# First loads on one queue and a newly searched instruction order in a fused attention and FFT kernel

## The chip, the cores and the metric

The kernel runs on one core of one Trainium2 chip. The metric is device microseconds (us) of one execution; lower is better. A run also reports the span from its first to its last instruction, some 2 us shorter than the time, and the mean clock that the throttle granted TensorE over that span (1.0 is full speed). That clock matters here: all differences in question are a few us, and one stretch of TensorE at half clock (3.41 us in these traces) costs about 1.7.

## The reference, cut to what matters

Branch A is compressive-memory attention: 32 heads of 20 columns, a sequence of 2048 rows in 4 segments of 512, softmax inside the segment and a linear memory from the segments before. Branch B is a 2-D FFT filter of its own input. A gate mixes the two.

```python
def _A_ref(x, wq, wk, wv, wo, beta):          # x: 1 x 2048 x 640, H = 32, N = 4 segments, L = 512
    ...
    for s in range(N):
        qs, ks, vs = (q[:, :, s].copy(), k[:, :, s].copy(), v[:, :, s].copy())
        logits = jnp.einsum('bhqd,bhkd->bhqk', qs, ks) * scale + mask
        p = _softmax(logits, axis=-1)
        a_dot = jnp.einsum('bhqk,bhkd->bhqd', p, vs)
        pq = phi(qs)
        num = jnp.einsum('bhld,bhde->bhle', pq, M)
        den = jnp.einsum('bhld,bhd->bhl', pq, z)[..., None] + 1e-06
        o = g * (num / den) + (1.0 - g) * a_dot
        ...
def _B_ref(x, w_r, w_i):
    X = rfft2(x) * (w_r + 1j * w_i)
    return irfft2(X)
...
g = _sigmoid((x * gate_w).sum(-1, keepdims=True))
return g * a + (1 - g) * b
```

## The kernel before

The program first records every operation (a matmul group, an eviction from PSUM, a mask, a DMA) with its inputs and outputs. A long list of integers, `ORDER`, then gives the order in which each engine issues its operations: entry `v` is operation `v // 2`, and `v % 2` picks one of up to two engines (or DMA queues) that may do it. Semaphore waits are made from the recorded dependences, so another list gives the same result, at another time. The list was found by an off-line search over a model of the durations (`QUEUE` has the model's issue and transfer times of DMAs in ns).

```python
    EARLY = ("ld_wqa", "ld_wka", "ld_wqb", "ld_wkb", "ld_wv", "ld_x", "ld_fcat", "ld_big", "ld_beta", "ld_gw", "ld_hm")
    ...
    def dma(self, dst, src, nbytes, r, w, prio, tr=False, name="", after=(), queue="sp"):
        ...
        queues = ("sp", "act") if name in self.EARLY else (queue,)
        return self.Sc.op({e: (f, cost, 0.0) for e in queues}, r=r, w=w, ...)

    def schedule(self, pools, order, nsem=56):
        for v in order:
            o = ops[v // 2]
            o.eng = list(o.alts)[v % 2]
            queue[o.eng].append(o)
        ...
    def warm_up(self):                       # ten dummy matmuls of 512 columns, before any data are there
        ...
        for k in range(self.NWARM):
            self.mms([(lambda k=k: (self.ps(bank, 0, [1, L]), t.ap(0, [1, P]), t.ap(P, [1, L]), True, True, {}), 1000)],
                     [b("warm"), bank], [], -1.0, name="warm")

    def mask(self, s, g, np_, d0, s0, n, rk, wk, prio, base, step=64):   # GpSimd, causal mask on the exp tile
        e0 = self.exo(s, g)
        self.one("pool", lambda e: e.affine_select(
            self.ex.ap(e0 + d0, [1280, 4], [1, n], np_=np_), self.ex.ap(e0 + s0, [1280, 4], [1, n], np_=np_),
            [[0, 4], [step, n // 64], [1, 64]], ALU.is_ge, 0.0, base=base, channel_multiplier=-1), ...)

    # filter of branch B: the product with the weights, added up by VectorE or GpSimd
    fn = lambda e, ...: e.tensor_tensor(Yt.ap(r * 322, [1, KD]), Pt.ap(a0 * 322, [1, KD]), Pt.ap(a1 * 322, [1, KD]), op)
    self.either(fn, KD, [...], [Yb[r]], prio2, name="W_add")
    # phi of branch A, in two steps on VectorE
    fmax = lambda e: e.tensor_scalar(dst(), qsl(), 0.0, 1.0, ALU.max, ALU.add)          # "phi_max"
```

The scores of the attention come in 92 units (a QK matmul group, then one exp on ACT). I use the starts of these 92 exps, numbered from 0, as milestones.

The softmax here doesn't subtract the row's maximum and nothing guards it: scores larger than these inputs give would overflow.

## Time and profile before

| | before |
|---|---|
| first measurement | 245.87 us median of 3 (243.79 to 251.13) |
| profiled span, clock | 244.7 us, 0.986 |
| TensorE, VectorE, ACT, GpSimd busy | 94%, 81%, 81%, 68% |

The prediction below shows the lines. Two things help in reading on. The profiled execution had one stretch of half clock, 208.3 to 215.2 us. And with 48 runs of this kernel on record with their clock at the end, its runs fall into classes by granted clock: mean span 241.6 us at 0.998 to 1.0 (12 runs), 243.3 at 0.992 to 0.993 (23), 245.0 at 0.985 to 0.986 (11; the five of them in the fast state have 244.6), 247.4 at 0.979 (2, both in the slow state). One window of 3.41 us at half clock takes 0.7% off the mean clock, and from class to class the span grows by about 1.7 us.

### The profile page before, as it was taken

Reading aid. Unit: us, or ns where it says so; the run is one execution under the profiler, and the core shown is the slowest. Engines: PE = TensorE matmul, PEld = TensorE weight load, DVE = VectorE, ACT = ScalarE, POOL = GpSimd, SP = SyncE. Lnnn points to the kernel's source line nnn. Section 1 sums busy time; section 2 is a strip of 40 time slices with the busy share of each in tenths; the row PEclk is TensorE's granted clock in tenths of the full one; section 3 lists DMA queues with packets and bytes.
Section 4 is the critical chain, followed back from the end, with each engine's and each line's share of the span. In section 5 each row is a group of like instructions: output and inputs, shape, how many; then the busy total and the mean of one; then the engine's idle time right before and its main releaser. Section 6 shows DMA issues by size and latency. Waiting matters only on the chain.

```text
span 244.7 us, 10242 instructions
## 1 busy us (share of the span) xinstructions
PE 229.2 (94%) x4347; PEld 141.3 (58%) x4361; DVE 197.3 (81%) x481; ACT 199.3 (81%) x241; POOL 166.5 (68%) x297
## 2 busy tenths in 40 slices
PE   7699999999989999999889999899989999899994
PEld 2476566765556565555546555455545556467794
DVE  0379998879899996898899798998988878635563
ACT  2089688889899999999889979999899978388730
POOL 8514259447959956938964999877899867459730
PEclk9999999999999999999999999999999999599999
DMA  7999859993998775494688571264676995722123
GB/s 174 297 348 206 198 165 175 288 195 100 169 285 175 169 220 147 100 240 89 224 211 250 151 233 50 99 175 138 183 221 198 237 180 101 112 54 86 56 85 108
DMA packets 58928, 42.17 MB, mean 172 GB/s; under 512 B 30020, under 2 KB 55172, under 8 KB 58884
## 3 DMA queue, kind: packets, MB, share of 16 engines
q1 hardware_dynamic: 56100, 39.72, 66.4%
q10 hardware_dynamic: 2784, 1.81, 2.9%
q8 instruction: 34, 0.56, 1.0%
q14 instruction: 10, 0.08, 0.1%
HBM read 23.32 MB, written 12.30 MB: 146 GB/s over the span
## 4 chain that ended last, share of the span: by engine, by line
PE 59%; DVE 14%; DMA 10%; ACT 9%; SPq 3%; issue 2%; ACTq 0%; DVEq 0%
PE psum L514 53%; PE psum L512 7%; ACT ex L1263 6%; DMA xT<-in_A_x_dram 3%; DMA pkn<-phk 2%; SPq L548 2%; DMA r<-r_scr 2%; DVE Pt L1439 2%; DMA qk_scr<-qu 2%; DMA r_scr<-rc 2%; SPq L546 1%; DVE G L1485 1%; DVE phk L1085 1%; DVE oU L1526 1%; ACT et L1072 1%
## 5 line engine op out<-in xcount | busy, mean ns | idle before, releaser
L1284 POOL TENSOR_SCALAR_AFFINE_SELECT ex<-ex 128x256 bf16<-128x256 bf16 (+2 forms) x224 | 122.1, 567 | 41.1 <-ACT ex L1263 37.7
L1263 ACT ACTIVATE ex<-psum 128x2048 bf16<-128x2048 f32 (+4 forms) x92 | 138.7, 1508 | 13.9 <-PE psum L514 12.0
L514 PE MATMUL psum<-qkp 20*64 20x64 bf16 (+5 forms) x1280 | 32.7, 272 | 2.2 <-ACT ex L1263 1.7
L514 PE MATMUL psum<-xT,wk 128*128 128x256 bf16 (+1 forms) x280 | 34.1, 276 | 0.2 <-issue 0.2
L514 PE MATMUL psum<-wv,xT 128*32 128x321 bf16 (+3 forms) x400 | 30.1, 301 | 0.6 <-DVE va L1115 0.3
L514 PE MATMUL psum<-xT,wq 128*128 128x512 bf16 (+1 forms) x121 | 27.5, 396 | 2.6 <-DMA xT<-in_A_x_dram 2.0
L1439 DVE TENSOR_TENSOR Pt<-psum,Wt 128x642 bf16<-128x642 f32 x32 | 25.5, 821 | 2.3 <-PE psum L514 2.1
L514 PEld LDWEIGHTS psum<-qkp 20*64 20x64 bf16 x1280 | 13.5, 103 | 19.5 <-ACT ex L1263 13.6
L514 PEld LDWEIGHTS psum<-xT,wk 128*128 128x128 bf16 (+1 forms) x280 | 20.1, 99 | 6.4 <-issue 0.8
L512 PE MATMUL psum<-wo,oU 128*32 128x320 bf16 x480 | 23.5, 319 | 0.0
L906 POOL TENSOR_TENSOR xsb<-xf 128x320 bf16<-128x320 bf16 (+2 forms) x12 | 9.3, 777 | 17.7 <-DVE xsb L906 13.3
L525 DVE CAST ot<-psum 128x320 bf16<-128x320 f32 x21 | 10.1, 491 | 12.6 <-PE psum L512 10.1
L514 PEld LDWEIGHTS psum<-wv,xT 128*32 128x32 bf16 (+1 forms) x400 | 14.3, 96 | 8.4 <-issue 3.1
L514 PE MATMUL psum<-big,Ac 128*128 128x160 bf16 (+2 forms) x96 | 18.1, 258 | 0.7 <-DVE Pt L1439 0.3
L1115 DVE TENSOR_TENSOR va<-psum,ebx 128x320 bf16<-128x320 f32 x32 | 15.2, 484 | 4.3 <-ACT gate L1113 2.1
L514 PE MATMUL psum<-big,Cp 128*128 128x321 bf16 (+1 forms) x96 | 18.0, 302 | 0.2 <-DVE G L1485 0.2
L514 PE MATMUL psum<-ex,va 128*32 128x64 bf16 (+3 forms) x576 | 17.4, 256 | 0.7 <-DVE dn L1152 0.3
L1485 DVE TENSOR_TENSOR G<-eo,psum 128x320 bf16<-128x320 f32 x32 | 14.7, 482 | 3.6 <-PE psum L514 2.6
L514 PEld LDWEIGHTS psum<-ex,va 128*32 128x32 bf16 x576 | 11.1, 96 | 9.7 <-POOL ex L1284 3.4
L514 PE MATMUL psum<-tt,Yt 128*128 128x256 bf16 (+1 forms) x96 | 16.4, 275 | 0.2
L1072 ACT ACTIVATE et<-qu 128x512 bf16<-128x512 bf16 x25 | 15.6, 629 | 0.1
L512 PEld LDWEIGHTS psum<-wo,oU 128*32 128x32 bf16 x480 | 12.6, 101 | 5.3 <-issue 1.3
(99 smaller groups left out, 393.5 us busy)
## 6 DMA issues: line engine op xcount, KB each, us to landing
qkp<-qk_scr SPq DMA_DIRECT2D x28, 160.0 KB
tt<-tab_tt SPq DMA_DIRECT2D x8, 512.0 KB, 4.3
qk_scr<-qu SPq DMA_DIRECT2D x12, 256.0 KB, 3.1
u_scr<-ub SPq DMA_DIRECT2D x12, 256.0 KB, 3.8
xsb<-in_A_x_dram SPq DMA_DIRECT2D x6, 320.0 KB, 6.3
oU<-u_scr SPq DMA_DIRECT2D x15, 128.0 KB, 2.7
out_dram<-ot SPq DMA_DIRECT2D x12, 160.0 KB
Wt<-in_B_w_r_dram SPq DMA_DIRECT2D x16, 80.2 KB, 2.6
```

Source lines behind the costliest of these rows:

```text
L512: h = e.matmul(dst, wt, r_, start=st, stop=sp_, **{**kw, "tile_position": (0, q), "skip_group_check": True})
L514: h = e.matmul(o_, l_, r_, start=st, stop=sp_, **kw)
L525: alts["dve"] = (lambda e: e.tensor_copy(dst(), src()), 67 + 1.04 * n, 68.0)
L546: return e.dma_start_transpose(d_, s_)
L548: return e.dma_start(d_, s_)
L906: self.either(lambda e, dst=dst, src=src, d0=d0, n=n, op=op: e.tensor_tensor(xs.ap(o + dst, [D, 2], [1, n]), xf.ap(src + d0, [321, 2], [1, ...
L1072: self.one("act", lambda e: e.activation(et.ap(0, [1, L]), qsl(), ACT.Exp), L, [qb], [b("et", pi_)], late, name="phi_exp")
L1115: self.one("dve", lambda e: e.tensor_tensor(va.ap(i * H * VW + h0 * VW, [VW, nh], [1, DH]), self.ps(bank, 0, [DH, nh], [1, DH]), self.ebx. ...
L1263: self.one("act", lambda e, d=d, q=q: e.activation(self.ex.ap(*d), self.ps(bank, *q), ACT.Exp, scale=SC), n, [bank], [self.exb(s, 2 * pr + ...
L1284: self.one("pool", lambda e: e.affine_select(self.ex.ap(e0 + d0, [1280, 4], [1, n], np_=np_), self.ex.ap(e0 + s0, [1280, 4], [1, n], np_=np_),
L1439: self.one("dve", lambda e, ri=ri, Pt=Pt, Wt=Wt, wo_=wo_, bank=bank: e.tensor_tensor(Pt.ap(ri * 322, [644, 2], [1, KD]), self.ps(bank, 0, ...
L1485: self.one("dve", lambda e, q=q, n2=n2, bank=bank, eo=eo: e.tensor_tensor(self.G.ap(n2 * D + 639 * q, [1 - 2 * q, 320]), eo.ap(q, [1, 320] ...
```

## The change

Its intent: let ACT's queue carry only the first half of wk and put all other first loads on SyncE's queue, in the order in which they are needed; correct the model's times of two transposes; search a new `ORDER` with these times.

```diff
-    EARLY = ("ld_wqa", "ld_wka", "ld_wqb", "ld_wkb", "ld_wv", "ld_x", "ld_fcat", "ld_big", "ld_beta", "ld_gw", "ld_hm")
+    EARLY = ("ld_wqa", "ld_wka")
     QUEUE = {
...
-        ... ("xT", 131072): (1260.0, 900.0, 16), ("xT", 262144): (1800.0, 1600.0, 16),
+        ... ("xT", 131072): (1240.0, 1300.0, 16), ("xT", 262144): (1700.0, 2300.0, 16),
...
     ORDER = (
-        47, 0, 90, 26, 74, 23, 2, 4, 37, 24, 6, 8, 28, 10, 12, 72, 14, 16, 30, 18, 20, 178, ...
+        25, 0, 74, 46, 22, 2, 4, 26, 6, 8, 10, 30, 12, 104, 90, 14, 93, 28, 72, 36, 44, 202, ...
         (2328 entries, nearly all at new places)
     )
```

## The prediction

> **What bounds the kernel now.** I read the page's busy table and slices first, then the chain of work that ended last, then the first 15 us of the timeline with their waits and windows, because that is where the named part of the change lies.
>
> ```profile
> span 244.7 us, 10242 instructions
> PE 229.2 (94%) x4347; PEld 141.3 (58%) x4361; DVE 197.3 (81%) x481; ACT 199.3 (81%) x241; POOL 166.5 (68%) x297
> ...
> PEclk9999999999999999999999999999999999599999
> DMA  7999859993998775494688571264676995722123
> ```
>
> No engine idles for long: TensorE is at 94%, ACT and DVE both at 81%. The reader should see two more things: the DMA engines are at nine tenths or more in the second to fourth slice (a slice is 6.1 us), and one slice near 210 us ran at about half the granted clock. That last one is noise for this question: in the windows table the clock was 0.92 in 200 to 210 us and 0.74 in 210 to 220 us, so about 0.8 + 2.6 = 3.4 us of TensorE time went to it in this execution, and three timed runs from 243.79 to 251.13 us fit such a thing coming and going.
>
> The chain of waits says what a changed beginning is worth:
>
> ```profile
> 0.78 1.24 SPq L546
> 2.08 0.56 SPq L548
> 2.70 1.71 SPq L546
> 4.45 6.75 DMA xT<-in_A_x_dram
> 11.25 11.24 PE psum L514 x171
> 22.54 7.38 PE psum L514 x55
> ```
>
> The last piece of the transposed x lands at 11.2 us. From then to 30 us TensorE works without a gap, and later in the chain it holds 59% of the span. So the arrival of that piece is on the path. The timeline shows who shares the DMA engines with it:
>
> ```profile
> 0.79 0.38 ACTq L548 DMA_DIRECT2D xsb<-in_A_x_dram  x1
> 1.20 0.46 ACTq L548 DMA_DIRECT2D wq<-in_A_wq_dram  x1
> 2.08 0.56 SPq L548 DMA_DIRECT2D wk<-in_A_wk_dram  x1
> 2.70 3.59 SPq L546 DMA_TRANSPOSE xT<-in_A_x_dram  x2
> 5.82 0.39 ACTq L548 DMA_DIRECT2D wk<-in_A_wk_dram  x1
> 6.25 0.54 ACTq L548 DMA_DIRECT2D xsb<-in_A_x_dram  x1
> 11.25 0.40 PE L514 MATMUL psum<-xT,wq 128*32 128x512 bf16 x4 [1.70 <-DMA xT<-in_A_x_dram]
> 12.57 1.57 ACT L523 ACTIVATE qkp<-psum 128x512 bf16<-128x512 f32 x3 [6.53 <-PE psum L514]
> ```
>
> At 5.82 and 6.25 us ACT's queue starts the large second half of wk (560 KB) and a 320 KB piece of x while the last transpose is still under way. TensorE waits 1.70 us for that transpose. After it come 1.92 us of matmuls, the four evictions into qkp, the first QK matmuls at 14.30 us and the first exp at 14.83 us. The windows give the load:
>
> ```profile
> 5.00:11.25 6.25, 4.27 (x75) 1.88 (x73) 2.36 (x5) 0.23 (x1) 4.41 (x7) 1.00 1.13 271
> 11.25:14.30 3.05, 3.05 (x59) 2.05 (x59) 1.91 (x4) 1.57 (x3) 0.24 (x1) 1.00 1.03 357
> ```
>
> The next to last column is the DMA share. It is above 1, so the engines are full, and the order of the bytes, not their number, decides when one piece lands.
>
> [...] wk's second half (issue to landing 5.2 us, so at about 11.0 us) is in before the transpose that was issued 1.4 us earlier and lands at 11.2 us. [...] a transpose issue costs 1.24 to 1.84 us and a plain load 0.4 to 0.6 us. [...] the ten warm-up matmuls take 4.45 us, 0.43 us each, which is 512 columns at half rate[...]. [...]
>
> **The change part by part.** (1) The queues. Before, ACT issued a piece of x, wq's first half, beta, wk's second half, another piece of x, and the gate weights. After, it issues only wk's first half (240 KB), and SyncE issues in this order: x piece 320 KB, wq first half 240 KB, transpose of chunk 0, transpose of chunks 3 and 4, transpose of chunks 1 and 2, then beta, x, wk's second half and the rest. Added up with issue times from the trace: 0.78 start + 0.38 + 0.46 + 1.24 + 1.71 + 1.84 + five gaps of 0.05 = 6.66 us for the end of the last transpose's issue, against 6.29 us before. That is 0.37 us lost. Chunk 0 starts at 1.70 instead of 0.78 us, 0.9 us lost, but before it wq (landed near 5.3 us) held the first matmul at 5.68 us as much as chunk 0 did.
>
> What is won: the bytes that must land by the last transpose are 328 + 246 + 246 + 655 + 8 = 1483 KB. Summing the windows from 1 to 11.25 us gives about 2480 KB moved, so some 1000 KB (wk's second half 573, x 328, fcat 98, all or in part) went in front. With 222 KB in by 3 us and 258 GB/s after, the mean of 3 to 10 us, the needed ones alone would be in at 7.9 us. The issue ends only at 6.66, and the middle transpose landed 3.2 us after its own issue ended under load, so I take 2.5 to 3.2 us after 6.66: 9.2 to 9.9 us, say 9.5 (an estimate). Saved: 11.2 - 9.5 = 1.7 us. A chunk's direct projections took 0.96 us, so the last two end near 11.5 us instead of 13.17. The evictions are split two and two over ACT and DVE in place of three and one, which takes about 0.3 us from the row of three that ran 12.57 to 14.14 us. Sum: first QK near 12.3 instead of 14.30 us, 2.0 us earlier, if the array is warm.
>
> (2) The warm-up. The new order runs 7 dummy matmuls and puts the other three between the first projections. Seven at 0.43 us are 3.0 us, from 1.3 to 4.3 us, then a gap until chunk 0 lands near 6 us. If this leaves the array at half rate, chunk 0 and the next one take up to 0.96 us more each. I charge half of that chance: 0.7 us. Gain at the first QK: 1.3 us.
>
> (3) The order. The same 1073 groups of matmuls stand in TensorE's list and QK units keep their order. Counting columns[...], the work left after the first QK starts is 183.0 us before and 184.1 us after; from the fifth QK unit it is 164.8 us in both, from the 41st 85.2 in both. So the first QK is only brought forward by postponing 1.1 us of projections, and TensorE was gapless in this stretch, so that 1.1 us comes back: 1.3 - 1.1 = 0.2 us net, or 0.9 us with a warm array. Tiling-mode changes go from 220 to 225. On ACT, after the first exp, there are three more projection evictions, one more each of D, F1 and pv, five more final ones, less two of Tb and oT3: by their row means (0.60, 0.54, 0.60, 0.60, 0.44, less 0.48 and 0.60) some 3.5 us more, most of it early or in the tail where ACT has slack; DVE has three instructions fewer.
>
> (4) The rest of the search. It removes no work. It can only remove waits, such as the chain's 4.05 and 4.66 us of r_scr and r at 196 to 205 us and short stalls between QK units; but the new order keeps the same TensorE distance from the last PV of segment 2 to the first output projection that needs it. I give the search 1.0 us. Sum: 245.87 - 0.5 (start, between 0.2 and 0.9) - 1.0 = 244.4 us.
>
> **The rivals.** First, all of the early 2 us survives and the search finds more in the middle: about 241 us. For it speaks the unbroken TensorE stretch in the chain; against it the equal work left from the fifth QK unit. Second, the gain is hidden: loads needed at 16 to 22 us (wv, wq's second half) land no earlier, since the engines are full until 20 us and the bytes ahead of wq's second half are the same 4858 KB in both, by adding up the loads in order of issue; the early time then becomes a gap and the result is 245.5 to 246. Third, one queue for everything: a SyncE instruction that waits holds all behind it. Before, the timeline shows this at 7.87 to 11.22 us, where SyncE waited 3.3 us for xT before issuing wv. With ACT's six loads moved to it, later stores could slip: 247 to 248.
>
> **Range and chances.** The structure gives -0.5, the search -1.0 with an uncertainty of 2 to 3 us, and the clock dip moves single runs by 3 us. So 244.4 us, 8 in 10 within 240.8 to 248.0. Two per cent faster would be below about 241, which needs the first rival: 0.12. Two per cent slower needs the third and a dip: 0.06. Within 2%: 0.82.
>
> **What would show it.** Right: the last xT lands between 9 and 10 us with wk's second half and x behind it; first exp before 13.5 us; the fifth QK unit (35.3 us for its exp now) less than 1.5 us earlier; TensorE's busy time equal within 2 us. The warm-up charge is right if the first projections run at 0.43 us per 512 columns. Wrong: a last xT still near 11 us (then the transpose itself, not the sharing, sets it), or a lead that grows beyond 2 us after 60 us, which would be the search's work in the middle that I could not size.

## The result, and the profile after

| | before | changed |
|---|---|---|
| median of the runs | 246.55 us (243.79 to 251.13, 4 runs) | 253.47 us (253.12 to 254.82, 4 runs) |
| ratio of fast runs | | 1.033, 95% interval 1.023 to 1.043 |
| profiled span, clock | 244.7 us, 0.986 | 251.4 us, 0.977 |

A ratio is the mean time of one kernel's fast runs over that of the other's fast runs of the same rounds, so it is not quite the ratio of the medians quoted. A run's state is called slow when it is over 1.5% above the fastest of the same kernel. Both kernels are correct. The change is slower by over 3%, outside the predicted range.

The page of the changed kernel (busy time, and the clock in 40 slices of 6.3 us):

```profile
span 251.4 us, 10251 instructions
...
PE 232.7 (93%) x4361; PEld 140.6 (56%) x4361; DVE 197.2 (78%) x478; ACT 201.1 (80%) x247; POOL 164.0 (65%) x294
...
PEclk9799999999999999999999999999999999599998
```

VectorE, ACT and GpSimd are busy nearly as long as before (197.3, 199.3 and 166.5 us there). The second digit of the clock row, 7, is new. The timeline of the changed kernel's first us:

```profile
1.31 3.17 PE L514 MATMUL psum<-G 128*128 128x512 bf16 x7 [1.31 <-DVE G L797]
...
6.43 0.40 PE L514 MATMUL psum<-xT,wq 128*32 128x512 bf16 x4 [1.95 <-DMA xT<-in_A_x_dram]
...
8.46 1.07 PE L514 MATMUL psum<-xT,wk 128*32 128x256 bf16 x16
```

Seven warm-up matmuls end at 4.48 us, then TensorE waits 1.95 us. Its windows cut at the borders of the trace's clock records (full from 4.38 to 7.79 us, half from 7.79 to 11.20, then full for 201.39 us, which is 59 times 3.413; the third column is TensorE's busy time, the third from the right the clock):

```profile
4.37:7.79 3.42, 1.47 (x16) 0.46 (x15) 0.00 (x0) 0.00 (x0) 3.42 (x2) 1.00 1.19 248
7.79:11.20 3.41, 3.41 (x49) 1.88 (x52) 0.16 (x1) 0.00 (x0) 3.11 (x5) 0.50 0.82 220
```

In the first window TensorE was busy 1.47 of 3.42 us (43%), and the next window ran at half clock, over the first projections. The first exp came at 14.22 us, only 0.61 before the 14.83 of the kernel before; e4 below tests whether the half clock is why.

The larger loss is later. The list of waits, TensorE's three longest in the changed kernel (total, number, longest):

```profile
PE psum L514 <- DVE Cp L525: 2.5, 1, 2.5
PE psum L514 <- issue: 2.2, 2, 1.4
PE psum L514 <- DMA xT<-in_A_x_dram: 2.0, 1, 2.0
```

and two of the kernel before (the one for Cp is not in its list):

```profile
PE psum L514 <- DMA xT<-in_A_x_dram: 2.0, 2, 1.7
...
PE psum L514 <- issue: 0.7, 4, 0.2
```

The wait for Cp is one event. The timeline of the changed kernel around it:

```profile
134.37 2.35 POOL L1284 TENSOR_SCALAR_AFFINE_SELECT ex<-ex 128x256 bf16<-128x256 bf16 x5
134.44 2.52 DVE L1444 TENSOR_TENSOR Yt<-Pt 128x321 bf16<-128x321 bf16 x1
136.88 1.60 DVE L1084 TENSOR_SCALAR phq<-qu 128x512 bf16<-128x512 bf16 x1
...
138.41 0.67 DVE L525 CAST Cp<-psum 128x512 bf16<-128x512 f32 x1
...
139.13 0.30 PE L514 MATMUL psum<-tt,Yt 128*65 128x256 bf16 x1 [2.55 <-DVE Cp L525]
```

and the same operations in the kernel before:

```profile
131.44 0.55 DVE L1444 TENSOR_TENSOR Yt<-Pt 128x321 bf16<-128x321 bf16 x2
...
132.36 2.30 POOL L1284 TENSOR_SCALAR_AFFINE_SELECT ex<-ex 128x256 bf16<-128x256 bf16 x5 [1.09 <-ACT ex L1263]
...
133.35 0.47 DVE L1084 TENSOR_SCALAR phq<-qu 128x512 bf16<-128x512 bf16 x1
...
134.16 0.69 DVE L525 CAST Cp<-psum 128x512 bf16<-128x512 f32 x1
```

VectorE's addition into Yt took 2.52 us instead of about 0.3 and the scaling into phq 1.60 instead of 0.47, while GpSimd's masks ran one after another beside them. The eviction Cp stands behind both on VectorE, and TensorE waited 2.55 us for it. From windows of both kernels, TensorE's busy time in 120 to 140 us:

```profile
120.00:140.00 20.00, 16.17 (x297) 10.71 (x290) 18.39 (x47) 16.55 (x20) 15.79 (x32) 1.00 0.54 164
```

```profile
120.00:140.00 20.00, 18.94 (x351) 11.92 (x350) 18.39 (x49) 18.40 (x20) 13.72 (x28) 1.00 0.70 195
```

The first is the changed kernel: 2.77 us less, with VectorE equally busy. So VectorE's "busy" here includes time in which it got little done (2.52 us for an addition of about 0.3). A third event is in the chain of waits of the changed kernel:

```profile
39.34 13.72 PE psum L514 x233
53.06 1.37 issue
54.43 7.86 PE psum L514 x94
```

TensorE stood still for 1.37 us at 53 us without a releaser that the profile shows.

How far each kernel lags behind the one before, at the start of exp number 0, 4, 12, 40, 44, 76 and 91 (differences of starts read from the traces, in us; a star: that profile had less half clock after 200 us than the two windows of the profile before, so its last column is too good by about 1.7 us a window; e9 had three windows there, so its last column is too bad by as much):

| kernel | 0 | 4 | 12 | 40 | 44 | 76 | 91 |
|---|---|---|---|---|---|---|---|
| changed, first profile | -0.61 | -0.03 | 1.28 | 1.97 | 4.62 | 7.03 | 6.19 |
| changed again (e16) | -0.65 | -0.05 | 1.49 | 2.42 | 6.62 | 8.93 | 8.43 |
| e1 new start, old rest | -0.39 | 0.60 | 0.46 | 0.10 | 0.10 | 0.47 | 0.51 |
| e2 old start, new rest | -0.36 | -0.25 | -0.39 | 0.30 | 2.94 | 5.29 | 5.36 |
| e3 old order, new queues | -0.29 | -0.29 | -0.33 | -0.29 | -0.29 | -0.30 | -0.29 |
| e4 changed, warm first | -1.92 | 0.17 | 0.26 | 0.95 | 3.60 | 5.90 | 4.91 |
| e5 new middle only | 0.31 | 0.57 | 0.34 | 0.57 | 5.13 | 6.91 | 4.25* |
| e6 new to the 45th | -1.04 | -0.22 | 1.33 | 2.05 | 6.04 | 6.45 | 3.76* |
| e7 collision undone | -0.70 | -0.12 | 1.18 | 1.87 | 2.25 | 4.65 | 4.29 |
| e8 collision put in | -0.44 | -0.43 | -0.57 | -0.86 | -0.53 | -0.53 | -3.22* |
| e9 thin masks | 0.70 | 1.28 | 1.54 | 2.27 | 2.35 | 4.73 | 5.35 |
| e10 three repairs | -1.83 | -0.10 | 1.68 | 2.40 | 2.69 | 3.03 | 0.34* |
| e13 four repairs | -0.41 | 0.17 | 0.67 | 1.37 | 1.62 | 1.93 | 1.88 |
| e11 old to the 45th, new tail | -0.21 | -0.21 | -0.23 | -0.73 | -0.72 | 1.65 | 1.40* |
| e12 old order, new queues, longer warm-up | -0.80 | -0.13 | -0.21 | -0.54 | -0.54 | -0.55 | -1.71* |
| e14 old to the 65th, new tail | -0.22 | -0.22 | -0.32 | -1.05 | -1.05 | 2.76 | 1.87* |
| e15 old to the 77th, new tail | 0.08 | 0.08 | -0.03 | -0.40 | -0.40 | -0.41 | -3.23* |
| e17 the same again | -0.05 | -0.05 | -0.31 | -0.66 | -0.66 | -0.66 | -4.09* |

The last rows show the scatter. e11, e14, e15 and e17 have the old order up to exp 40 and read -0.40 to -1.05 there, so the one profile of the kernel before is itself some 0.7 us late at that point, and a level under about 0.7 us says little. The steps after exp 40 are steadier: e15 and e17 change by 0.01 from 40 to 76.

### The profile page after: what moved, and what is told of

Its sections match the earlier page's. It is cut to its first block, busy times and chain, and to the rows that moved or that the text cites.

```text
span 251.4 us, 10251 instructions
## 1 busy us (share of the span) xinstructions
PE 232.7 (93%) x4361; PEld 140.6 (56%) x4361; DVE 197.2 (78%) x478; ACT 201.1 (80%) x247; POOL 164.0 (65%) x294
## 4 chain that ended last, share of the span: by engine, by line
PE 69%; DVE 15%; ACT 5%; DMA 3%; issue 3%; POOL 2%; SPq 1%; DVEq 0%; ACTq 0%
PE psum L514 62%; PE psum L512 8%; ACT ex L1263 4%; DVE Pt L1439 4%; DVE Yt L1444 2%; POOL ex L1284 2%; DMA xT<-in_A_x_dram 2%; DVE G L1485 1%; DMA oU<-u_scr 1%; DVE Cp L525 1%; DVE phq L1084 1%; DVE mem L1157 1%; DVE phk L1085 1%; DVE dn L1155 1%; DVE ot L525 1%
## 5 line engine op out<-in xcount | busy, mean ns | idle before, releaser
L1284 POOL TENSOR_SCALAR_AFFINE_SELECT ex<-ex 128x256 bf16<-128x256 bf16 (+2 forms) x224 | 120.8, 564 | 45.6 <-ACT ex L1263 43.0
L514 PE MATMUL psum<-xT,wq 128*128 128x512 bf16 (+1 forms) x135 | 31.5, 402 | 2.3 <-DMA xT<-in_A_x_dram 2.0
L514 PE MATMUL psum<-wv,xT 128*32 128x320 bf16 (+3 forms) x400 | 29.8, 301 | 0.2 <-ACT Ac L523 0.2
L514 PE MATMUL psum<-tt,Yt 128*128 128x256 bf16 (+1 forms) x96 | 16.6, 274 | 4.0 <-DVE Cp L525 2.5
L514 PE MATMUL psum<-big,Cp 128*128 128x321 bf16 (+1 forms) x96 | 19.5, 308 | 0.7 <-DVE G L1485 0.3
L514 PE MATMUL psum<-big,Ac 128*128 128x161 bf16 (+2 forms) x96 | 18.6, 257 | 1.4 <-issue 1.4
L906 POOL TENSOR_TENSOR xsb<-xf 128x320 bf16<-128x320 bf16 (+2 forms) x11 | 8.4, 772 | 15.4 <-DVE xsb L906 15.2
L525 DVE CAST ot<-psum 128x320 bf16<-128x320 f32 x16 | 7.5, 489 | 12.9 <-PE psum L512 6.9
L514 PEld LDWEIGHTS psum<-xT,wq 128*128 128x128 bf16 (+1 forms) x135 | 9.5, 100 | 10.5 <-DMA wq<-in_A_wq_dram 2.8
L512 PEld LDWEIGHTS psum<-wo,oU 128*32 128x32 bf16 x480 | 11.9, 99 | 6.2 <-issue 3.1
```

The lines of the kernel that those rows point to most:

```text
L512: h = e.matmul(dst, wt, r_, start=st, stop=sp_, **{**kw, "tile_position": (0, q), "skip_group_check": True})
L514: h = e.matmul(o_, l_, r_, start=st, stop=sp_, **kw)
L525: alts["dve"] = (lambda e: e.tensor_copy(dst(), src()), 67 + 1.04 * n, 68.0)
L906: self.either(lambda e, dst=dst, src=src, d0=d0, n=n, op=op: e.tensor_tensor(xs.ap(o + dst, [D, 2], [1, n]), xf.ap(src + d0, [321, 2], [1, ...
L1284: self.one("pool", lambda e: e.affine_select(self.ex.ap(e0 + d0, [1280, 4], [1, n], np_=np_), self.ex.ap(e0 + s0, [1280, 4], [1, n], np_=np_),
```

## The experiments

After the first result I held this theory, M: the new order loses its time in the middle, after 40 us, above all in the event at 137 us. The rival, S: the start (half clock, postponed projections, the one queue) loses it, and what follows is its echo.

All kernels of these experiments differ from one of the two in `ORDER` alone unless I say so (e4, e7, e9, e10 and e13 also have the long `EARLY` of the kernel before, but their entries put the loads on the same queues as in the changed kernel). That an interval can leave out 1 by a draw of clocks alone is shown by e15 and e17. Two orders are joined like this: the first as far as the k-th QK unit, then whatever is not yet placed, in the sequence of the other.

```diff
-ORDER = NEW
+ORDER = NEW[:place of the 5th QK unit] + [v for v in OLD if v // 2 is not yet placed]     # e1
+ORDER = OLD[:place of the 5th QK unit] + [v for v in NEW if v // 2 is not yet placed]     # e2
```

**e1, the new start with the old rest; e2, the mirror.**

> The new order up to the fifth QK unit (about 35 us), then the old order for all that is left. Theory M (the loss is made in the middle of the new order, after 40 us): within 1% of before, so 0.99 to 1.01; the first exp near 14.2 us and the clock dip at 7.8 us as in the new kernel, and the lag behind before stays under 1 us at the 42nd exp. Theory S (the changed start, with its clock dip and its loads, leaves a deficit that grows): 1.02 to 1.035, and the lag at the 42nd exp is over 3 us.

> The mirror image: the old order and the old queues up to the fifth QK unit, then the new order. Theory M: 1.02 to 1.035 of before, with a gap of TensorE of over 1.5 us near 137 us behind a DVE addition into Yt that takes over 1.5 us. Theory S: 0.99 to 1.01.

Measured: e1 246.65 us median against 245.06 (ratio 1.006, interval 1.000 to 1.012); e2 252.98 us (1.032, 1.026 to 1.039). Nearly the whole loss goes with the new rest; S falls as the main cause. In the table e2 is level with before up to exp 40 and jumps by 2.6 us between 40 and 44, where the changed kernel does.

**e3, the old order on the new queues; e4, the changed kernel with all ten warm-up matmuls ahead of everything else on TensorE.**

```diff
 # e3: OLD order, first loads on SyncE; ACT keeps the first half of wk and beta; chunks 1, 2 of xT ahead of 3, 4
 # e4: NEW order, the three late warm-up entries moved up
-        25, 0, 74, 46, 22, 2, 4, 26, 6, 8, 10, 30, 12, 104, 90, 14, 93, 28, 72, 36, 44, 202, 16, 34, 18, 48, ..., 52, 20,
+        0, 2, 4, 6, 8, 10, 12, 14, 16, 18, 20, 25, 74, 46, 22, 26, 30, 104, 90, 93, 28, 72, 36, 44, 202, 34, 48, ..., 52,
```

> The queue change by itself: the old order on all compute engines, the first loads on SyncE's queue in the new sequence but with chunks 1 and 2 before 3 and 4, ACT's queue with wk's first half and beta only. By the prediction's own step the last xT lands at 9.2 to 9.9 us instead of 11.2 and the first exp comes 1.0 to 2.0 us before 14.83; the end 0 to 1.5 us earlier (ratio 0.994 to 1.0). The rival (the transposes set their own pace) has the last xT at 10.5 us or later and the first exp within 0.5 us.

> The new kernel with all ten warm-up matmuls first, as in the old one. If the idle gap at 4.5 to 6.4 us is what took the clock to half at 7.8 us, the dip is gone or starts elsewhere, the first exp comes 0.7 to 1.7 us earlier than 14.22, and theory M lets only a part of it reach the end (252.0 to 253.3 us against 253.5). Theory S lets it reach the end and more (below 251).

Measured: e3 245.29 us (0.999, 0.992 to 1.006), e4 253.88 us (1.036, 1.028 to 1.044). The queue change alone costs and wins nothing. Its start missed the expectation: the last piece of xT landed at 8.53 us instead of 11.21, yet the first exp came only 0.29 us earlier, the rival's mark. TensorE has no wait over 0.15 us between 6.72 us and that exp, but its clock was half until 10.1 us (four 512-column matmuls on a piece of xT took 0.67 us at 8.38 us and 0.40 at 10.96; in the profile before it was half until 6.95). In e4 the clock is full from 6.95 us and the start is as early as hoped, first exp at 12.91. The timeline of e4 shows its last wait for a transposed piece:

```profile
8.53 0.40 PE L514 MATMUL psum<-xT,wk 128*32 128x256 bf16 x8 [0.83 <-DMA xT<-in_A_x_dram]
```

But the lead of 1.92 us is a lag of 0.17 at exp 4, which fits projections that were only postponed. And the time is no better. So half clock at the start is real, and not why the change is slow.

**e5, the new order only from the 33rd to the 45th QK unit; e6, the new order up to the 45th, the old after it.**

> The order of before up to the 33rd QK unit, then the changed order up to the 45th, then the order of before again; load constants of before. Theory L (one collision of VectorE with GpSimd's masks near 137 us, which lies in this segment, takes 2.6 of the lost us): exp number 41 (counted from 0) lags before by 2.3 to 3.0 us, the lag stays to the end, ratio to before 1.009 to 1.013. Rival D (the loss is spread evenly over the new order): this segment is an eighth of the units and loses under 1 us, ratio under 1.004.

> The changed order, with its load constants, up to the 45th QK unit, the order of before afterwards. Theory L with a smaller second part: lag at exp 44 about +4.6 us (or +2.9 if the late 1.4 us stall near 54 us does not recur), and it stays within 0.5 us of that to the end, ratio 1.011 to 1.019. Rival: the loss after the 45th unit is a consequence of being late there (a phase that no longer fits), then the lag still grows by 1 us or more and the ratio is over 1.02.

Measured: e5 250.27 us against 245.29 (1.018, 1.011 to 1.025), e6 251.04 (1.021, 1.014 to 1.028). Both lost more than I expected. Twelve of 92 units bring 1.8% alone, so the evenly spread loss falls. In e5 the addition into Yt took 3.93 us (it got through only during a second train of masks) and TensorE waited 3.10 us. In both, the window with the stall had TensorE busy 37% and 29%, and the next window, 3.41 us, ran at half clock: the stall costs another 1.5 us or so. That makes the lag at exp 44 5.13 and 6.04 us. In e5 one more VectorE instruction, at 147.2 us, took 2.47 us for 0.41 beside masks and cost another 1.8 us.

**e7, the collision undone in the changed kernel; e8, an attempt to put it into the kernel before.**

```diff
 # e7, VectorE's sequence in the changed kernel (1306: addition into Yt, 3346: scaling into phq, 1353: eviction Cp)
-  ..., 1346, ..., 1306, 3346, 1353, ...
+  ..., 1306, 1346, ..., 1353, 3346, ...
 # e8, in the kernel before: the addition next to the scaling, into the run of masks
-  ..., 1306, ..., 3346, ...
+  ..., 1306, 3346, ...            # 1306 moved down by six instructions
```

> The changed kernel with two VectorE instructions moved: the addition W_add into Yt that stood at 134.44 us goes ahead of the one at 132.60, and the scaling phq<-qu that stood at 136.88 goes behind the eviction Cp that stood at 138.41. Nothing else. Theory L: neither of the two instructions stands on VectorE's way to that eviction while GpSimd's masks run, the TensorE gap of 2.55 us before the matmul of 139.13 shrinks to under 0.6, the jump at exp 41 falls from 2.6 to under 0.8 us, and the end comes 1.5 to 2.5 us earlier than in the changed kernel: ratio to before 1.022 to 1.028. Rival (the stall only moves to the next user of the late chain): the jump or an equal one within five units stays, ratio over 1.029.

> The kernel before with one VectorE instruction moved: the addition W_add into Yt that ran at 131.44 us (0.31 us) goes behind the mem<-psum,dn of 132.94, next to the scaling phq<-qu of 133.35, where twelve of GpSimd's masks run one after another. Nothing else. Theory L: one of the two takes 1.5 us or more, the eviction Cp of 134.16 comes that much later, TensorE gets a gap of over 0.7 us near 135 us and the end is 0.7 to 2.5 us later, ratio 1.003 to 1.010. Rival (the duration belongs to the instruction or the surroundings of the changed kernel, not to the meeting of the two engines): durations under 0.6 us and ratio 0.998 to 1.002.

Measured: e7 251.99 us (1.025, 1.019 to 1.031). Its timeline:

```profile
132.51 0.54 DVE L1444 TENSOR_TENSOR Yt<-Pt 128x321 bf16<-128x321 bf16 x2
...
135.87 0.69 DVE L525 CAST Cp<-psum 128x512 bf16<-128x512 f32 x1 [1.44 <-PE psum L514]
136.48 0.54 DVE L1084 TENSOR_SCALAR phq<-qu 128x512 bf16<-128x512 bf16 x1
```

Now VectorE waits for TensorE instead, TensorE has no gap there, and the step from exp 40 to 44 is 0.4 us instead of 2.6. It did not come back later. e8 came out at 244.86 us (0.997, 0.990 to 1.004) and has no later lag, a miss for the simple form of my theory (its step from exp 40 to 44 is 0.33 us). Its timeline:

```profile
131.50 2.94 POOL L1284 TENSOR_SCALAR_AFFINE_SELECT ex<-ex 128x256 bf16<-128x256 bf16 x6 [1.09 <-ACT ex L1263]
...
132.49 0.48 DVE L1444 TENSOR_TENSOR Yt<-Pt 128x321 bf16<-128x321 bf16 x1
132.89 0.54 DVE L1084 TENSOR_SCALAR phq<-qu 128x512 bf16<-128x512 bf16 x1
```

The same two instructions met a train of twelve masks (the view ends within it) and lost only 0.16 and 0.26 us against their medians of 0.32 and 0.28. So a meeting of the two engines can cost 0.2 us or several; it isn't enough to stall. Did the masks cause the long one at all, or only lie beside it?

**e9, nine masks made thin.** VectorE's order stays as in the changed kernel; the masks between 134.4 and 139.4 us treat one of four column groups (meant to give a wrong result).

```diff
+        self.mk = getattr(self, "mk", -1) + 1
+        q = 1 if self.mk in (104, 107, 105, 108, 106, 101, 103, 109, 111) else 4
-            self.ex.ap(e0 + d0, [1280, 4], ...), self.ex.ap(e0 + s0, [1280, 4], ...), [[0, 4], [step, n // 64], [1, 64]], ...
+            self.ex.ap(e0 + d0, [1280, q], ...), self.ex.ap(e0 + s0, [1280, q], ...), [[0, q], [step, n // 64], [1, 64]], ...
```

> The changed kernel in its own order; only nine of GpSimd's 224 masks, those that ran between 134.37 and 139.4 us, treat a quarter of their columns (wrong result on purpose). VectorE's order is untouched, so the addition into Yt that took 2.52 us still meets them. Theory L (VectorE is kept out while these masks run one after another): each of the five masks ahead takes about 0.25 to 0.4 us instead of 0.45 to 0.67, the addition takes 0.3 to 1.6 us, the TensorE gap of 2.55 us falls under 1.6 us, exp 41 jumps by under 1.6 us. Rival W (the addition waits for something else, its inputs or the write of an engine, and the masks only lie beside it): 2.3 us or more and a gap over 2.3 us.

```profile
134.67 1.25 POOL L1286 TENSOR_SCALAR_AFFINE_SELECT ex<-ex 128x64 bf16<-128x64 bf16 x5
134.74 0.36 DVE L1446 TENSOR_TENSOR Yt<-Pt 128x321 bf16<-128x321 bf16 x1
135.01 0.35 DVE L1084 TENSOR_SCALAR phq<-qu 128x512 bf16<-128x512 bf16 x1
```

The addition starts 0.07 us after the first mask, exactly as in the changed kernel, and takes 0.36 us; the gap of TensorE is gone, and exp 40 to 44 costs 0.08 us. The rival, that it waits for its inputs, falls: the masks kept it out. In the changed kernel it took 2.52 us and ended at 136.96 us, 0.24 after the last of five masks in a row; by what the masks keep it out, no run shows. The time, 251.68 us (1.031, 1.026 to 1.036), moved less than e7's, with a profile in which the clock became full only at 12.8 us. From both runs, the collision is worth 2.2 to 2.6 us in a trace. The ratios (1.025 and 1.031 against 1.033 and 1.034) suggest 0.5 to 2 us, but their intervals overlap with those of the changed kernel: what the repair saves in time is not clear of noise.

**e10, three repairs: warm-up first, collision undone, old order from the 45th unit. e11, only the new tail. e12, the old order on the new queues with a longer warm-up.**

```diff
 # e10
-ORDER = NEW
+ORDER = (e4 with the moves of e7)[:place of the 45th QK unit] + [the rest in OLD's sequence]
 # e11
+ORDER = OLD[:place of the 45th QK unit] + [the rest in NEW's sequence]
 # e12, on top of e3
-             self.mms([(lambda k=k: ..., 1000)], [b("warm"), bank], [], -1.0, name="warm")
+             self.mms([(lambda k=k: ..., 1000)] * (3 if k > 6 else 1), [b("warm"), bank], [], -1.0, name="warm")
```

> The changed kernel with three repairs at once: all ten warm-up matmuls first, the collision near 137 us undone, and the order of before from the 45th QK unit on. If the losses are separate terms that add (about 1.3 us from the half clock at 8 to 11 us, 2.2 to 2.6 from the collision, 2.1 to 2.7 from the new order after the 45th unit), what is left is under 1.5 us: lag at exp 40 about +0.9, at 44 +0.6 to +1.4, at 91 the same apart from the late clock dip; ratio 1.000 to 1.008. Rival: one loss stands in for another (a repaired place lets a later wait end last), ratio over 1.012.

> The order of before up to the 45th QK unit, the changed order after it, load constants of before. If the changed order loses 1.5 to 2.7 us by itself in this part, lag 0 at exp 44, +0.5 to +0.9 at 52 to 60, +1.3 to +1.8 at 64, +1.5 to +2.5 at the end, ratio 1.006 to 1.011. Rival (the later loss follows from coming late to the 45th unit): lag under 0.7 us at the end and ratio under 1.003.

> The order of before with nearly all first loads on SyncE's queue (as in the earlier run of that kind), and the last three of the ten warm-up matmuls doubled and tripled to sixteen in all, so that no gap opens before the first transposed piece of x at 6.7 us. If the clock is full from 7 us and the lead at the first exp is kept as the small one of 0.3 us was: first exp 13.0 to 13.7 us, lag -1.0 to -1.8 from exp 4 to the end, ratio 0.993 to 0.996. Rival (hidden: the lead is gone at exp 4, because loads needed between 16 and 22 us land no earlier): ratio 0.998 to 1.002.

e10: 249.03 us against 245.08 (1.016, 1.009 to 1.023), worse than expected. The table says where: flat after exp 44, as expected, but 2.40 us late by exp 40. Its timeline:

```profile
41.22 1.81 SPq L548 DMA_DIRECT2D qk_scr<-qu  x1
...
45.60 0.60 ACT L523 ACTIVATE qu<-psum 128x512 bf16<-128x512 f32 x1 [1.55 <-DMA qk_scr<-qu]
...
46.26 0.34 PE L514 MATMUL psum<-fcat,xsb 128*128 128x128 bf16 x3 [1.46 <-ACT gate L1113]
```

SyncE issues without pause from 35 to 48 us in the changed order. The store of qu, whose data are ready from 35 us, stands behind two loads of Wt; its issue took 1.81 us instead of 0.60, ACT's next eviction into the same buffer waited 1.55 us for it, and TensorE 1.46 us for the gate evictions behind that. The profiles of e6 and e7 have the same stall (1.50 and 1.24 us), those of the changed kernel, e4 and e9 do not. In the changed kernel's first profile the long issue met a transpose right behind that store instead (2.31 us, at 39.89 us).

e11: 248.67 us (1.021, 1.015 to 1.028), more than I expected; at a clock of 0.993 its mean span is 246.6 us (3 runs) against 243.3, 3.3 us. The new tail loses by itself. I looked for waits there, but the windows from exp 44 to 76 of e8 (old tail) and e11 say otherwise (second and third number: length and TensorE's busy time):

```profile
141.56:203.25 61.69, 58.93 (x1141) 33.36 (x1143) 54.51 (x135) 56.83 (x66) 51.74 (x93) 1.00 0.64 170
```

```profile
141.37:205.43 64.06, 60.97 (x1146) 33.13 (x1145) 56.67 (x138) 56.33 (x63) 49.97 (x92) 1.00 0.60 153
```

Of the 2.37 us that e11 takes longer, TensorE is idle for 0.33 and counted as busy for 2.04. In the same windows the groups of matmuls on Cp and Ac with the table `big` fill 18.0 and 5.5 us instead of 16.6 and 4.7, with 92 and 24 instructions for 90 and 24, while the mean duration of one is the same (304 and 257 ns, 303 and 258): they overlap with others less. Why was not tested. e12: 246.20 us (1.007, 1.001 to 1.014): first exp at 14.03 us only, since TensorE then waits 1.07 us for wk's second half, which the new queue order sends later (issued at 6.97 us, 5.82 before), and the lead is gone at exp 4. Its rival, the hidden gain, holds; at equal clock it is level with before (243.2 us, 3 runs at 0.993).

**e13, e10 with that one store ahead of the two loads of Wt. e14 and e15, the old order up to the 65th and up to the 77th unit, new after it. e16, the changed kernel again.**

```diff
 # e13, SyncE's sequence (1956: the store of qu, 934: the first of the two loads of Wt)
-  ..., 934, ..., 1956, ...
+  ..., 1956, 934, ...
 # e14, e15
+ORDER = OLD[:place of the 65th (77th) QK unit] + [the rest in NEW's sequence]
```

> The three repairs of before and one more: SyncE's store of qu that was issued at 41.22 us in that run (and took 1.81 us to issue instead of 0.60), and for which ACT's next eviction into qu waited 1.55 us and TensorE 1.46 us, goes ahead of the first of the two loads of Wt before it. Its data are ready from about 35 us. Theory S2 (what is left of the loss is SyncE's full stretch of issuing: a store with work waiting for it stands behind loads that nobody needs yet): no TensorE gap over 0.6 us between 40 and 56 us, lag at exp 8 under 1.2 instead of 2.3 us, at exp 40 and 76 about 1.0 to 1.5 instead of 2.4 and 3.0, ratio 1.004 to 1.011. Rival (the delay of SyncE only meets another instruction, and TensorE has its gap there): a gap of over 1 us elsewhere before 60 us, ratio over 1.013.

> The order of before up to the 65th QK unit, the changed order after it. The kernel with the changed order from the 45th unit on lost about 3.3 us (span 246.5 against 243.2 at the same granted clock of 0.993). If half of it lies before the 65th unit, this one loses 1.2 to 2.2 us, ratio 1.004 to 1.009. If all lies in the last part (projection of the output and the last stall of 1.28 us): ratio over 1.011; if none: under 1.003.

> The order of before up to the 77th QK unit, the changed order after it. Only the last 15 units and the output projection are the changed ones: if the late stall before an output projection (1.28 us in one run, 0.48 us in the changed kernel) belongs to them, 0.5 to 1.5 us are lost, ratio 1.001 to 1.006, else 0.998 to 1.002.

> The changed kernel itself, as a control beside the other runs of this call: 252.5 to 254.5 us, ratio 1.027 to 1.038; the stall of 2.5 us near 137 us as in the first profile, and the 1.2 to 1.5 us stall between 41 and 55 us at one of its two places.

e13: 247.55 us against 245.54 (1.010, 1.004 to 1.016), a ratio as expected; the times alone do not separate it from e10 (1.016, 1.009 to 1.023). The delay of SyncE is still there, but meets a load that nobody needs yet:

```profile
40.33 2.02 SPq L548 DMA_DIRECT2D Wt<-in_B_w_r_dram  x1
...
45.12 0.28 PE L514 MATMUL psum<-fcat,xsb 128*128 128x128 bf16 x2 [0.32 <-ACT gate L1113]
```

The lag is 1.37 us at exp 40 and 1.9 from 76 to the end (1.0 to 1.5 expected). Its start shows that ten warm-up matmuls first are no sure repair: the clock was halved again from 8.70 to 12.11 us, and the first exp came only 0.41 us early. In e10, e13 and e16 a 16 KB packet of instructions was under way on its own queue when SyncE's long issue began (from 40.9, 40.2 and 40.6 us); that it causes the delay is a guess, not tested.

e16: 254.20 us (1.034, 1.026 to 1.043), and its profile (span 253.6) has both losses at once: the store's stall of 1.48 us and the collision of 2.55 us, after which the clock was halved. Its windows there:

```profile
136.30:139.72 3.42, 0.87 (x10) 0.59 (x7) 3.42 (x4) 1.35 (x2) 3.42 (x7) 1.00 0.54 145
139.72:143.13 3.41, 3.41 (x26) 1.80 (x25) 2.04 (x4) 1.88 (x1) 0.13 (x1) 0.50 0.34 85
```

TensorE was busy 0.87 of 3.42 us, and the next window ran at half clock: exp 40 to 44 cost 4.2 us there, 1.6 more than in the first profile, where the same gap fell across two windows (TensorE busy 2.48 and 1.78 of 3.41 us).

e14: 249.94 us (1.016, 1.007 to 1.024), a miss upwards; its one run at full clock has a span of 245.5 against 241.6 us. e15: 243.59 us (0.992, 0.985 to 0.999). So the new order of the last 15 units loses nothing. It would be rash to put the tail's loss into units 65 to 77: in e14's trace the lag grows by 3.8 us from exp 60 to 76 (one window of half clock at 188 us has up to 1.7 of it), and two TensorE gaps of 1.45 and 1.55 us at 213 and 219 us follow where e15 has one of 0.78, but in e11 the lag grows by 1.67 us from exp 44 to 64 and by 0.70 from 64 to 76. Joining the lists adds losses of its own. After exp 44 the new order changes TensorE's tiling mode 114 times instead of 107; what one change costs, no run shows.

**e17, e15 again.** Was e15 a version that beats both?

> The same kernel as in the earlier run with the order of before up to the 77th QK unit and the changed order after it, which came out at 0.992 with three of four runs at a granted clock of 0.999 to 1.0, where 7 of 32 runs of the kernel before had such a clock. If the changed last part gains by itself (its TensorE gap near 209 us is 0.78 instead of 1.46 us), ratio 0.990 to 0.996 again and runs of equal clock 0.5 to 0.8 us apart. If the earlier result was a lucky draw of clocks: ratio 0.997 to 1.003, and at equal clock the spans agree within 0.4 us.

Measured: 244.36 us (1.002, 0.996 to 1.008). At full clock the eight runs of e15 and e17 have a mean span of 242.0 us, twelve of the kernel before 241.6. The 0.992 was a draw of clocks. (The "7 of 32" of the expectation is 7 of 36.) No version here beats the kernel before.

## Why the prediction was wrong

*Step 1, the queues: right in direction.* The first matmul on data came at 6.43 us, and with a warm array (e4: full clock from 6.95 us) the last wait for a piece of xT ended at 8.53 us, earlier than the 9.2 to 9.9 estimated; e4's first exp was 1.92 us earlier, 2.0 predicted for a warm array. That the two agree is partly luck: the last piece landed 2.7 us earlier (8.47 against 11.21), not 1.7. That ACT's late loads had held it up by taking bandwidth was my estimate; no run isolates it.

*Step 2, the warm-up: right in direction, too small.* That the gap would leave TensorE at half clock was my estimate; in the changed kernel a wait of 1.95 us was followed by half clock from 7.79 to 11.20 us. The charge of 0.7 us (half of twice 0.96 would have been 0.96) measured 1.31 in one pair of profiles (first exp 14.22 us in the changed kernel, 12.91 in e4). It varies: against the kernel before, the first exp stood between -1.04 and 0.70 us with seven warm-up matmuls first (e6, e9), and at -1.92, -1.83 and -0.41 with ten (e4, e10, e13). "First exp before 13.5 us" failed for this. It did not decide the time: e4 is no faster.

*Step 3, what the order postpones: right in sign.* The term of 1.1 us measured 2.1: e4's lead of 1.92 at exp 0 is a lag of 0.17 at exp 4. The net start gain, 0.2 to 0.9 us, was nil, and e3 confirms that the queues by themselves give nothing (0.999).

*Step 4, "The rest of the search. It removes no work. It can only remove waits": this failed.* I credited 1.0 us. The new rest alone (e2) makes 1.032. The sentence is half true: an order removes no work, but it can also add waits, and make the same matmuls overlap less; I had no way to see either from the list. I checked counts and distances in TensorE's list, where all was equal. At equal clock (0.985 to 0.986) the changed kernel's span is 6.7 us over the one before in fast runs (251.3 and 244.6 us, 2 and 5 runs); the rest of the 7 to 9 us between the medians goes with the lower clocks of its runs. The parts shown:

- VectorE kept out by GpSimd's masks at 137 us: a gap of 2.55 us on TensorE's path, shown by removing it in two ways (e7, e9), and in three profiles some 1.5 us more with a halved clock after it (e5, e6, e16).
- A store of qu behind loads on SyncE: 1.24 to 1.50 us in four of the seven profiles of the new order with its new start (e6, e7, e10, e16), shown in the trace by moving that store (e13). It is of the kind of the third rival, one queue for everything, but not by the loads that were moved to SyncE: both loads of Wt were on its queue before. And it is not needed for the result: e2 has no such stall and still loses 3.2%. In the first profile there is a stall of 1.37 us at 53 us instead, whose cause stays open.
- The new order after the 45th unit: 3.3 us (e11, at equal clock), 2.4 us of lag from exp 44 to 76 in the changed kernel itself, and nothing after the 77th (e15, e17). Most of it is no wait but TensorE busy longer with nearly the same matmuls (e11 against e8: 2.04 of 2.37 us). The cause of that stays open.

The collision and the tail together make nearly the whole: e2, which has both and the old start, is at 250.7 us (3 runs at 0.984 to 0.986), 6.1 over the kernel before. But the terms do not add exactly: with the warm-up, the collision and the store repaired and the old tail, 2.1 us at equal clock are left (e13: 245.4 us in 4 runs at 0.993, against 243.3), whose cause stays open.

*The rivals.* The first (all of the early gain survives) was wrong. The second (hidden) is what the new start does when the old rest follows it: 1.006. *The range* allowed 2 to 3 us for the search, in both directions of a small gain; the true error was about 7, from 1.0 us credited to some 6 lost, and the 0.06 given to a slowdown of 2% needed the third rival and a dip. *The clock* was judged rightly: the changed kernel's loss isn't a dip, and single runs move by 3 us with it. The test "TensorE's busy time equal within 2 us" failed by the profile (229.2 and 232.7 us; 231.2 in e4, which has no half clock at the start), but it was too fine for it: 14 matmul records are missing from the profile before (4347 against 4361).

## What to carry to other kernels

An order that a search finds on modelled durations must be judged on the chip, stretch by stretch: cut the old and the new list at a milestone, join the halves both ways, and look at which half carries the loss before explaining anything. Look then for instructions that are long only in one kernel (here 2.52 us for 0.3) and ask which other engine worked beside them, for all of that time counts as busy. TensorE's busy time has to be read with the same care: two lists of nearly the same matmuls differed by 2.04 us of it and by only 0.33 us of idle time (e11 against e8). And on a DMA queue that issues without pause, put first the stores that free a buffer, and loads that nobody awaits behind them (TensorE waited 1.46 us in e10 and 0.32 in e13).

## What the runs show of the chip, and what they leave open

- Beside GpSimd's masks a VectorE instruction took several times its usual time, or nearly its usual time. The addition into Yt (median 0.32 us) took 2.52 us over five masks in a row (changed kernel), 3.93 us over two trains of masks (e5) and 0.36 us beside thin masks (e9); in e8 it and the scaling into phq lost only 0.16 and 0.26 us by a like train. What decides between these, the runs do not tell.
- Half clock followed windows of 3.41 us in which TensorE was partly busy: 25% (e16), 29% (e6), 37% (e5), 43% (changed kernel) and 45% (e7, e13), and not those with 46% (e2, 133 us), 48% (e15, 9.5 us) and 52% (changed kernel, 137.5 us). The late half clock of the next point is another case.
- The cause of the late half clock is not shown: in 12 of 19 profiles TensorE ran at half rate for one to three windows beginning at 208 to 215 us (in a thirteenth, e14, at 188 us), in 11 of them after 198 to 205 us at full rate without a break, though it had been busy 77% to 83% in the window before (58% in e12); in e8 a window at 66% there was not followed by one, nor was one at 76% at 123 us in the kernel before. Each such window costs about 1.7 us, and their number goes with most of the spread of the times.
- In some profiles an issue on SyncE's queue took 1.2 to 1.5 us longer than usual (1.81 and 2.02 us for 0.60 and 0.49, in e10 and e13); the cause is not shown. What it costs depends on what stands there: TensorE waited 1.46 us in e10 and 0.32 in e13.
